# Attention and a gated MLP on one core: q without zero padding, w_in converted in halves throughout, and two slices of w_in loaded through ScalarE's DMA queue

## The chip, the cores and the metric

One core of a Trainium2 chip runs the whole program in one launch. The metric is device microseconds of an execution; the median of three executions stands for the kernel. Engines are called as in the profile: PE (TensorE), PEld (its weight loads), DVE (VectorE), ACT (ScalarE), POOL (GpSimd) and SP (SyncE, which here only issues DMAs).

## The reference

q, k and v are 4 batches x 12 heads x 448 positions x 64. The attention is causal; its output, as 1792 tokens x 768, goes through a gated MLP with w_in (768 x 2048) and w_out (2048 x 768). Both weights arrive as 64-bit floats, q, k and v as 32-bit ones; the output is float32.

```python
scores = scale * np.matmul(q, k.transpose(0, 1, 3, 2))
scores = np.where(mask, -1000000000.0, scores)
attn = np.exp(scores - np.max(scores, axis=-1, keepdims=True))
attn = attn / (np.sum(attn, axis=-1, keepdims=True) + 1e-09)
x = concat_heads(np.matmul(attn, v))
h = x @ w_in
g = h * (1.0 / (1.0 + np.exp(-1.702 * h)))
out = g @ w_out
```

## The kernel before

**Work.** Each batch's 448 positions are cut into blocks of 256 and 192 (eight blocks in all), each block into chunks of 64 positions. A *unit* is a block and a pair of heads: six units to a block. For each unit, scores of each chunk go to PSUM on TensorE (`scores_of`, L1071), DVE adds the mask and takes the row's minimum of the negated scores (L1112), ACT takes the exponential (L1126), the weights are scaled by the reciprocal of their sum, turned, and multiplied with v (L1268) into xT. Then comes the MLP of that block: `h_slice` (L412 with ps_h) over eight slices of w_in of 256 columns, the gate on ACT and DVE, and `out_tile` (L1405) with w_out. MLP products take each operand as a high and a low half-precision part, so w_in and w_out are converted and split on the chip.

**The first batch in float32.** For batch 0 the six units of both blocks work in float32 (`f32`, L853). `q_unit32` (L917) and `k_unit32` (L900) load two heads as 128 (or 96) rows, TensorE turns them into ps_o (`turn`, L885, matmuls at L893), and a copy by ACT or DVE (`scaled`, L472 or L474) brings them to SBUF. In kT the two heads lie in the upper and lower 64 partitions, copied at once. In qT each head has its own 64 columns of a 128-wide group, and the other head's half of these partitions is zero: four memsets (L934) write the zeros once, and each unit needs two copies of 64 partitions. The scores of a chunk are then a product over all 128 partitions, issued by `halves` (L408 to L412) as two matmuls of 64 stationary columns each, the zeros removing the other head. A run of two chunks shares a PSUM bank if it has at most 512 columns; the first block of a batch has two such groups for a unit, the second three (320, 384 and 448 columns).

**w_in.** `w_in_slice` (L632) loads a slice of 64-bit words in two DMAs of 768 KB on SP's queue (L648), into one of two raw buffers in wob (slices s and s + 2 share one). `to_f32` (L551) turns it into float32 with four operations: a scaling on ACT (L472), two 16-bit operations on DVE (L574, which may run on ACT as L566, and L588), and one on DVE (L599) that reads the raw words for the last time. The first three slices (`early=3`) do this in two halves, each after its own DMA; the others in one piece after both. Then follow the products of a slice with itself on TensorE, a maximum, a scale, and the split into two parts (L472 or L474, and L477).

**Order.** Every instruction is added to `Ops` with a price, its engine or engines of choice, and a priority. `Ops.order` searches 600 times, starting from a seed, for the order in each engine's queue with the least planned time (`forward`, `backward` and `late`), with prices such as `LOAD` for the issue of a DMA on SP, and the program is then emitted in that order. All loads go through SP's one queue, in the planned order. `warm` (L529) makes ACT load its table at the start.

The planner's price for the float32 scores, which the change leaves, is

```python
add({"PE": (4 * o / 2.4 + 6 * len(run)) / 1e3}, scores32, [qt_key] + kt_keys, bank(sb), prio)
```

with o the columns of the group, in nanoseconds for both halves together.

Of the kernel before, what the change touches and what calls it, by code (L numbers as in the profile page):

```python
# [11 lines left out]
F32 = mybir.dt.float32  # L12
# [36 lines left out]
    va=2,  # L49
    ub=(0.0, 60.0, 122.92, 9.75),  # L50
    wi2=2.63,
    early=3,
)

SEED = 2


class Ops:
# [5 lines left out]

    ENGINES = ("SP", "PE", "ACT", "DVE", "POOL")
    HOP = 0.14
    SECOND = 1e5
    LOAD = 0.68  # L70
    DMA_START, DMA_END, DMA_DEPTH = 1.23, 1.6, 8
    ROWS = 0.195

# [50 lines left out]
    def late(self, result, rnd):  # L124
        free = dict.fromkeys(self.ENGINES, 0.0)
        end = [0.0] * len(self.ops)
        bus, flying, clock = 0.0, [], Clock()
        for i, e in result:
            costs, _, deps, _, dma = self.ops[i]
            start = max([free[e]] + [end[d] + self.HOP for d in deps])  # L130
            if e == "SP":
                start = max([start] + flying[-self.DMA_DEPTH :][: len(flying) // self.DMA_DEPTH][:1])
                free[e] = start + costs[e]
                bus = max(bus, start + self.DMA_START) + dma
                end[i] = bus + self.DMA_END + 0.8 * rnd.random()
                flying.append(end[i])
                continue
            if e == "PE":
                end[i] = clock.after(start, costs[e])
            else:  # L140
                end[i] = start + costs[e] * (1 + 0.03 * rnd.random()) + (0.15 * rnd.random() if e == "POOL" else 0.0)
            free[e] = end[i]
        return max(free.values())

    def backward(self, found, spread, rnd):
        _, result, fin = found
        n = len(self.ops)
        on = dict(result)
        key = [-fin[i] - (rnd.gauss(0.0, spread) if spread else 0.0) for i in range(n)]
        wait, left = [0] * n, [0.0] * n  # L150
        for o in self.ops:
            for d in o[2]:
                wait[d] += 1
        ready = {e: [] for e in self.ENGINES}
        free = dict.fromkeys(self.ENGINES, 0.0)
        coming = [(0.0, i) for i in range(n) if not wait[i]]
        heapify(coming)
        at, now, done = [0.0] * n, 0.0, 0
        while done < n:
            while coming and coming[0][0] <= now + 1e-9:  # L160
                _, i = heappop(coming)
                heappush(ready[on[i]], (key[i], i))
            moved = False
            for e in self.ENGINES:
                if free[e] > now + 1e-9 or not ready[e]:
                    continue
                _, i = heappop(ready[e])
                costs, _, deps, _, dma = self.ops[i]
                left[i] = free[e] = now + costs[e]
                if e == "SP":  # L170
                    free[e] = now + max(costs[e], dma)
                    left[i] = now + self.DMA_START + dma + self.DMA_END + 0.3
                moved = True
                done += 1
                for d in deps:
                    at[d] = max(at[d], left[i] + self.HOP)
                    wait[d] -= 1
                    if not wait[d]:
                        heappush(coming, (at[d], d))
            if not moved:  # L180
                times = [free[e] for e in self.ENGINES if free[e] > now + 1e-9 and ready[e]]
                if coming:
                    times.append(coming[0][0])
                now = max(min(times), now)
        end = max(left)
        return [end - x for x in left]

    def forward(self, prios):
# [8 lines left out]
        coming = [(0.0, i) for i in range(n) if not wait[i]]  # L197
        taken = [None] * n
        free = dict.fromkeys(self.ENGINES + ("BULK",), 0.0)
        bus = 0.0  # L200
        clock = Clock()
        flying = []
        at = [0.0] * n
# [2 lines left out]
        while len(result) < n:  # L206
# [8 lines left out]
            for e in ("BULK",) + self.ENGINES:  # L215
# [11 lines left out]
                free[e] = end = now + costs[e]  # L227
                if e == "PE":
                    free[e] = end = clock.after(now, costs[e])
                if e == "SP":  # L230
                    go = max([now] + flying[-self.DMA_DEPTH :][: len(flying) // self.DMA_DEPTH][:1])
                    free[e] = go + costs[e]
                    bus = max(bus, go + self.DMA_START) + dma
                    end = bus + self.DMA_END
                    flying.append(end)
                    free["BULK"] = max(free["SP"], bus - TUNE["slack"])
# [76 lines left out]
def kernel(  # L313
# [76 lines left out]
    def col(tag, n=2, w=1):  # L390
        if tag not in col_at:
            col_at[tag] = (col_used[0], Ring(n))
            col_used[0] += n * w
            assert col_used[0] <= 175
        o, ring = col_at[tag]
        i = ring.next()
        return cols[:, o + i * w : o + (i + 1) * w], ("col", tag, i)
# [133 lines left out]
        nc.scalar.activation(out=cols[:, 175:], in_=cols[:, 175:], func=AF.Exp)  # L531

    add(dve(1), lambda e: nc.vector.memset(cols[:, 175:], 0.0), [], ["warm"], -2e6)
    add({"ACT": 1.5}, warm, [], ["warm"], -2e6)

    def zero_v(prio):
        add(
# [94 lines left out]
    def w_in_slice(s, prio):  # L632
# [11 lines left out]
        src = w_in32[:, 2 * s * WS : 2 * (s + 1) * WS].rearrange("(k p) f -> p k f", p=P)  # L644
        for h in range(2):
            add(
                {"SP": Ops.LOAD},
                lambda e, h=h: nc.sync.dma_start(  # L648
                    out=raw.bitcast(I32).rearrange("p (k w) -> p k w", k=NU)[:, 3 * h : 3 * h + 3],
                    in_=src[:, 3 * h : 3 * h + 3],  # L650
                ),
# [203 lines left out]

    ident = cp.tile([P, P], F32, name="ident")
    ident_keys = ["ident"]
    stale = [True] * 2
    ps_t_r = Ring(2)

    def identity(e):
# [55 lines left out]
    def q_unit32(n, u, prio):  # L917
# [6 lines left out]
        load_heads(f, q[b, 2 * u : 2 * u + 2, 64 * c0 : 64 * c1], r, [[x] for x in keys], prio, 0.062 * ni)  # L924
        got, got_key = turn(f, r, keys, prio)
        t = qT_r.next()
        qt = qT[t].rearrange("p c w -> p (c w)").bitcast(F32).rearrange("p (c j w) -> p c j w", j=2, w=64)
        key = ("qT", t)
        if stale[t]:
            stale[t] = False  # L930
            for j in range(2):
                add(
                    {"POOL": 0.4},
                    lambda e, j=j: nc.gpsimd.memset(qt[64 * j : 64 * j + 64, :, 1 - j], 0.0), [], [key], prio - 1,  # L934
                )
        for j in range(2):
            add(
                {**act(64 * ni, psum=True, rate=1.0), **dve(64 * ni)},
                lambda e, j=j: scaled(
                    e,  # L940
                    qt[64 * j : 64 * j + 64, :ni, j].rearrange("p c (x t) -> p c x t", t=2),
                    got[64 * j : 64 * j + 64].rearrange("p (c x) t -> p c x t", c=ni),
                    1.0,
                ),
                [got_key], [key], prio,
            )
        return qt[:, :ni], key, -QK_SCALE, None

    def k_pair(b, u, prio):

# [101 lines left out]
    def q_unit(n, u, prio):  # L1052
# [4 lines left out]
        if u % 2 == 0:  # L1057
            q_pair(n, u, prio)
        t, m = qT_r.next(), u % 2
        stale[t] = True  # L1060
        add(
            Ops.turned(2 * ni),
            lambda e: nc.sync.dma_start_transpose(out=qT[t][:, : 2 * ni], in_=q16[:, m * 256 * ni : (m + 1) * 256 * ni]),
# [7 lines left out]
    def scores_of(n, u, run, qt, qt_key, prio):  # L1071
# [8 lines left out]

        def scores32(e):
            for i, ps in zip(run, places):
                halves(ps, qt[:, i - c0].rearrange("p j w -> p (j w)"), kt[:, : 64 * (i + 1)], True, True)

        def scores(e):
            for i, ps in zip(run, places):
# [410 lines left out]
    moe(NB - 1)  # L1497

    with tc.manual_schedule():
        for i, e in ops.order():  # L1500
            ops.ops[i][1](e)


# [30 lines left out]
```

## Time and profile before

| | |
|---|---|
| three executions | 603.63, 605.53, 605.74 us (median 605.53) |
| the profiled execution | 605.29 us, its span 603.5 us |
| busy share of the span | PE 95%, PEld 83%, DVE 69%, ACT 58%, POOL 10% |
| granted TensorE clock, mean | 0.994 |
| DMA | 79.90 MB, mean 132 GB/s |

The times are of executions without and with a profile; the span runs from the first to the last instruction. A matmul's end is modelled, so that a busy PE may still have gaps inside; idle time of PE is real. The DMA share of a stretch is the mean over 16 DMA engines and can come out a little above 1. In the rows below, "idle" with an arrow names what ended the wait.

### The profile page before, as it was taken

What the parts mean: (1) busy time and instruction counts of PE and PEld (TensorE: products, weight loads), DVE (VectorE), ACT (ScalarE), POOL (GpSimd) and SP (SyncE); (2) the same over time, 40 slices, a digit from 0 to 9 for tenths busy, and PEclk for the clock granted to TensorE, in tenths of its full rate; (3) what the DMA queues carried; (4) which work ended last, traced back from release to release, by engine and by line L of the source; (5) the groups of instructions that cost most, each with busy time, mean ns of one, the idle gap of its engine ahead of it and who ended that gap; (6) DMA issues with size and microseconds to landing.
All of it is one profiled execution on the core that took longest, in us unless ns stands there. A gap on an engine that the chain in (4) does not pass through costs nothing.

```text
span 603.5 us, 22259 instructions
## 1 busy us (share of the span) xinstructions
PE 575.1 (95%) x9526; PEld 501.7 (83%) x9526; DVE 416.6 (69%) x1164; ACT 351.6 (58%) x835; POOL 59.2 (10%) x162
## 2 busy tenths in 40 slices
PE   3876999999999999999999999999999999999997
PEld 2555867886699799977888899998999999889986
DVE  2999999999996889977489887978777122203100
ACT  4888899887866767754676465666355122203110
POOL 3000000012120121212111210211100000000000
PEclk9989899999999999999999999999999999999999
DMA  8998478554498987899997899575835400000000
GB/s 270 277 288 281 128 251 302 173 127 110 86 177 156 142 163 112 167 176 153 156 158 115 155 161 174 105 128 120 130 59 68 94 2 15 1 28 3 28 28 27
DMA packets 201604, 79.90 MB, mean 132 GB/s; under 512 B 182304, under 2 KB 191264, under 8 KB 201504
## 3 DMA queue, kind: packets, MB, share of 16 engines
q1 hardware_dynamic: 201504, 78.47, 61.5%
q8 instruction: 74, 1.21, 0.9%
q14 instruction: 26, 0.21, 0.1%
HBM read 41.68 MB, written 5.51 MB: 78 GB/s over the span
## 4 chain that ended last, share of the span: by engine, by line
PE 68%; DVE 4%; ACT 2%; DMA 1%; issue 1%; SPq 0%; DVEq 0%; ACTq 0%
PE ps_o L1405 33%; PE ps_h L412 26%; PE ps_s L1089 4%; PE ps_v L1268 4%; DVE z L1112 1%; DMA vraw<-in_v_dram 1%; ACT p L472 1%; PE ps_s L412 1%; DVE p L477 1%; PE ps_h L883 1%; DVE ps_h L1367 0%; ACT waste L462 0%; DMA kf<-in_k_dram 0%; DVE q L477 0%; DVE gT L477 0%
## 5 line engine op out<-in xcount | busy, mean ns | idle before, releaser
L412 PE MATMUL ps_h<-xT,wib 128*64 128x256 f16 (+1 forms) x4608 | 244.4, 260 | 0.1
L1405 PE MATMUL ps_o<-wob,gT 128*64 128x384 f16 x2688 | 239.8, 326 | 0.8 <-DVE wob L477 0.6
L412 PEld LDWEIGHTS <-wib 128*64 128x64 f16 x4608 | 226.3, 110 | 7.9 <-issue 2.1
L1405 PEld LDWEIGHTS <-gT 128*64 128x64 f16 x2688 | 171.8, 110 | 38.3 <-issue 3.2
L1126 ACT ACTIVATE z<-z,cols 128x320 f32<-128x320 f32 (+6 forms) x168 | 84.1, 501 | 51.6 <-DVE cols L1112 49.1
L1367 DVE SCALAR_TENSOR_TENSOR ps_h<-t,ps_h 128x512 f32<-128x512 f32 (+1 forms) x64 | 40.1, 626 | 82.4 <-ACT t L1362 82.0
L1362 ACT ACTIVATE t<-ps_h,cols 128x512 f32<-128x512 f32 (+1 forms) x64 | 40.3, 629 | 72.1 <-PE ps_h L412 68.0
L1112 DVE CUSTOM_DVE_ANT_0 z<-ps_s,mask,cols 128x128 f32<-128x128 f32 (+6 forms) x126 | 57.2, 479 | 18.0 <-PE ps_s L1089 17.4
L477 DVE SCALAR_TENSOR_TENSOR p<-z,cols,p 128x128 f16<-128x128 f32 (+3 forms) x126 | 63.2, 528 | 1.5 <-ACT p L472 0.8
L477 DVE SCALAR_TENSOR_TENSOR gT<-ps_h,gT 128x512 f16<-128x512 f32 (+1 forms) x64 | 39.7, 620 | 13.5 <-ACT gT L472 13.1
L1268 PE MATMUL ps_v<-PT,v 128*64 128x192 f16 (+7 forms) x792 | 44.7, 257 | 0.5 <-DVE cols L453 0.4
L1089 PE MATMUL ps_s<-kT,qT 128*64 128x64 f16 (+4 forms) x504 | 41.5, 273 | 1.2 <-DVE cols L1112 0.9
L472 ACT ACTIVATE p<-z,cols 128x384 f16<-128x384 f32 (+3 forms) x66 | 34.0, 533 | 13.3 <-DVE cols L1235 9.7
L472 ACT ACTIVATE gT<-ps_h 128x512 f16<-128x512 f32 (+1 forms) x53 | 28.9, 545 | 20.4 <-DVE ps_h L1367 20.3
L472 ACT ACTIVATE ob<-ps_o,cols 128x384 f32<-128x384 f32 x24 | 13.8, 577 | 45.0 <-PE ps_o L1405 44.6
L1126 ACT ACTIVATION_READ_ACCUMULATOR z<-z,cols 128x1 f32 x168 | 31.6, 188 | 0.0
L412 PE MATMUL ps_s<-kT,qT 128*64 128x320 f32 (+6 forms) x168 | 25.0, 409 | 5.6 <-DVE cols L1112 5.6
L1268 PEld LDWEIGHTS <-v 128*64 128x64 f16 x648 | 29.2, 110 | 1.0
L1089 PEld LDWEIGHTS <-qT 128*64 128x64 f16 x504 | 24.7, 110 | 4.3 <-issue 1.3
L1047 POOL TENSOR_SCALAR q<-q 128x512 f16<-128x512 f16 (+1 forms) x32 | 21.9, 686 | 50.8 <-ACT q L472 26.6
L474 DVE TENSOR_SCALAR p<-z,cols 128x256 f16<-128x256 f32 (+3 forms) x60 | 24.6, 422 | 1.3
L472 ACT ACTIVATE wob<-wob 128x768 f32<-128x768 f32 (+1 forms) x20 | 21.8, 1091 | 5.5 <-DMA wob<-in_moe_w_in_dram 5.0
(98 smaller groups left out, 564.9 us busy)
## 6 DMA issues: line engine op xcount, KB each, us to landing
wob<-in_moe_w_in_dram SPq DMA_DIRECT2D x16, 768.0 KB, 6.5
wob<-in_moe_w_out_dram SPq DMA_DIRECT2D x9, 768.0 KB, 6.2
vraw<-in_moe_w_out_dram SPq DMA_DIRECT2D x7, 768.0 KB, 6.7
out_dram<-ob SPq DMA_DIRECT2D x28, 192.0 KB, 2.2
kf<-in_k_dram SPq DMA_DIRECT2D x36, 112.0 KB, 3.3
vraw<-in_v_dram SPq DMA_DIRECT2D x9, 384.0 KB, 5.0
qf<-in_q_dram SPq DMA_DIRECT2D x48, 64.0 KB, 3.1
qf<-in_q_dram SPq DMA_DIRECT2D x48, 48.0 KB, 3.2
```

The source lines that it names most:

```text
L412: nc.tensor.matmul(out[o : o + 64], lhsT[:, o : o + 64], rhs, start=start, stop=stop)
L472: nc.scalar.activation(out=dst, in_=src, func=AF.Copy, scale=sc)
L474: nc.vector.tensor_scalar(out=dst, in0=src, scalar1=sc, scalar2=None, op0=ALU.mult)
L477: nc.vector.scalar_tensor_tensor(out=dst, in0=src, scalar=sc, in1=hi, op0=ALU.mult, op1=ALU.subtract)
L1047: nc.gpsimd.tensor_scalar(out=dst, in0=src, scalar1=1.0, scalar2=1.0, op0=ALU.mult, op1=ALU.mult)
L1089: nc.tensor.matmul(ps[64 * j : 64 * j + 64], qt[:, g, i - c0, 64 * j : 64 * j + 64], kt[:, : i + 1, 64 * j : 64 * j + 64], start=(g == 0), ...
L1112: lambda e: nc.vector.tensor_tensor_reduce(out=z[:, :w], in0=ps, in1=mask[:, S - w :], scale=c, scalar=3.0e38, op0=ALU.add, op1=ALU.min, a ...
L1126: lambda e: nc.scalar.activation(out=z[:, :w], in_=z[:, :w], func=AF.Exp, bias=m, scale=-1.0, accum_out=l),
L1268: nc.tensor.matmul(ps[64 * j : 64 * j + 64, 64 * (first - c0) : w], vt[:, J, j] if f32(b, u) else vt[:, gv, J, j, :], (p_f32(pi)[:, at] if ...
L1362: lambda e: nc.scalar.activation(out=th, in_=ph, func=AF.Tanh, scale=ts[:, sl : sl + 1]),
L1367: lambda e: nc.vector.scalar_tensor_tensor(out=ph, in0=th, scalar=1.0, in1=ph, op0=ALU.add, op1=ALU.mult),
L1405: nc.tensor.matmul(po[64 * j : 64 * j + 64, :OH], gT[:, f, gg, 64 * r : 64 * r + 64], wo_pair(f, gw, nh), start=(f == 0 and gg + gw == 0), ...
```

## The change

- The q of the float32 units loses its zeros: qT holds the two heads in the upper and the lower 64 partitions, as kT does, copied at once for all 128 partitions. The memsets and the `stale` flags go. The scores of a chunk are two matmuls over 64 partitions each, one for a head: partitions 0 to 63 to the PSUM partitions 0 to 63, and 64 to 127 to 64 to 127.
- `early` goes from 3 to 8: all slices of w_in are converted in halves.
- The loads of the first two slices of w_in (`beside=2`, four DMAs) are issued by ACT on its own DMA queue, ahead of everything else. The planner gets this queue as an engine AQ, with `BESIDE` as the factor on transfers while both queues are at work. The price of `warm` grows by the four issues.
- `LOAD` goes from 0.68 to 0.5 and the seed from 2 to 3; the order is searched anew.

```diff
-    early=3,
+    early=8,
+    beside=2,
...
-SEED = 2
+SEED = 3
...
-    LOAD = 0.68
+    LOAD = 0.5
+    BESIDE = 1.4
...
+            if e == "AQ":
+                free[e] = start + costs[e]
+                side = max(side, start + self.DMA_START) + self.BESIDE * dma
+                end[i] = side + self.DMA_END + 0.8 * rnd.random()
+                continue
...
-                bus = max(bus, start + self.DMA_START) + dma
+                bus = max(bus, start + self.DMA_START)
+                bus += dma * (self.BESIDE if bus < side else 1.0)
...
-    add({"ACT": 1.5}, warm, [], ["warm"], -2e6)
+    add({"ACT": 1.5 + 2 * Ops.LOAD * TUNE["beside"]}, warm, [], ["warm"], -2e6)
...
-                {"SP": Ops.LOAD},
-                lambda e, h=h: nc.sync.dma_start(
+                {"AQ" if s < TUNE["beside"] else "SP": Ops.LOAD},
+                lambda e, h=h: (nc.scalar if e == "AQ" else nc.sync).dma_start(
...
-        qt = qT[t].rearrange("p c w -> p (c w)").bitcast(F32).rearrange("p (c j w) -> p c j w", j=2, w=64)
+        qt = qT[t].rearrange("p c w -> p (c w)").bitcast(F32)[:, : 64 * ni]
         key = ("qT", t)
-        if stale[t]:
-            stale[t] = False
-            for j in range(2):
-                add(
-                    {"POOL": 0.4},
-                    lambda e, j=j: nc.gpsimd.memset(qt[64 * j : 64 * j + 64, :, 1 - j], 0.0), [], [key], prio - 1,
-                )
-        for j in range(2):
-            add(
-                {**act(64 * ni, psum=True, rate=1.0), **dve(64 * ni)},
-                lambda e, j=j: scaled(
-                    e,
-                    qt[64 * j : 64 * j + 64, :ni, j].rearrange("p c (x t) -> p c x t", t=2),
-                    got[64 * j : 64 * j + 64].rearrange("p (c x) t -> p c x t", c=ni),
-                    1.0,
-                ),
-                [got_key], [key], prio,
-            )
-        return qt[:, :ni], key, -QK_SCALE, None
+        add(
+            {**act(64 * ni, psum=True, rate=1.2), **dve(64 * ni, rate=1.2)},
+            lambda e: scaled(e, qt.rearrange("p (x t) -> p x t", t=2), got, 1.0),
+            [got_key], [key], prio,
+        )
+        return qt, key, -QK_SCALE, None
...
-                halves(ps, qt[:, i - c0].rearrange("p j w -> p (j w)"), kt[:, : 64 * (i + 1)], True, True)
+                for j in range(2):
+                    x = slice(64 * j, 64 * j + 64)
+                    nc.tensor.matmul(
+                        ps[x], qt[x, 64 * (i - c0) : 64 * (i - c0) + 64], kt[x, : 64 * (i + 1)], start=True, stop=True
+                    )
...
-        for i, e in ops.order():
+        for i, e in sorted(ops.order(), key=lambda x: x[1] != "AQ"):
```

## Rows read from the trace of the kernel before

**Rows 1.** Busy us of each engine by stretch: (x instructions), TensorE clock, DMA share, GB/s

```profile
0.00:5.00 5.00, 0.00 (x0) 0.00 (x0) 0.06 (x1) 1.49 (x2) 3.84 (x20) 1.00 0.45 128
5.00:10.00 5.00, 1.80 (x10) 1.04 (x10) 1.47 (x3) 2.50 (x4) 0.71 (x4) 1.00 1.07 333
10.00:15.00 5.00, 3.49 (x28) 2.92 (x30) 2.45 (x8) 3.19 (x6) 0.00 (x0) 1.00 1.05 349
15.00:64.50 49.50, 38.09 (x520) 27.33 (x518) 47.21 (x146) 40.33 (x103) 0.00 (x0) 0.94 0.96 288
64.50:200.00 135.50, 132.88 (x2186) 108.77 (x2184) 125.15 (x333) 115.59 (x249) 13.57 (x31) 1.00 0.68 162
200.00:590.00 390.00, 388.74 (x6674) 353.32 (x6670) 240.25 (x677) 187.34 (x472) 41.07 (x109) 1.00 0.57 100
590.00:603.50 13.50, 10.04 (x124) 8.34 (x120) 0.00 (x0) 1.16 (x2) 0.00 (x0) 1.00 0.09 30
```

**Rows 2.** The timeline of the first 15 us: start, us, engine, line, operation

```profile
0.80 0.87 SPq L875 DMA_DIRECT2D q<-in_k_dram  x2
...
1.72 0.43 SPq L648 DMA_DIRECT2D wob<-in_moe_w_in_dram  x1
...
2.19 0.96 SPq L875 DMA_DIRECT2D qf<-in_q_dram  x2
...
6.76 0.89 ACT L472 ACTIVATE wob<-wob 128x768 f32<-128x768 f32 x1 [4.47 <-DMA wob<-in_moe_w_in_dram]
...
7.26 1.12 PE L893 MATMUL ps_o<-ident,qf 128*64 128x128 f32 x8 [7.26 <-DMA qf<-in_q_dram]
...
8.42 0.42 DVE L474 TENSOR_SCALAR qT<-ps_o 64x256 f32<-64x256 f32 x1 [7.49 <-PE ps_o L893]
...
11.04 1.11 PE L893 MATMUL ps_o<-ident,q 128*64 128x128 f32 x6 [1.05 <-DMA q<-in_k_dram]
...
14.55 0.23 DVE L1112 CUSTOM_DVE_ANT_0 z<-ps_s,mask 128x64 f32<-128x64 f32 x1 [1.96 <-PE ps_s L412]
```

**Rows 3.** Instructions on the tile qT: duration min/median/max in ns

```profile
L472 ACT ACTIVATE qT<-ps_o x17: 303/327/380, 8.9 to 112.2; 64x192 f32<-64x192 f32 x9, 64x256 f32<-64x256 f32 x8
L474 DVE TENSOR_SCALAR qT<-ps_o x7: 350/399/428, 8.4 to 54.6; 64x256 f32<-64x256 f32 x4, 64x192 f32<-64x192 f32 x3
```

**Rows 4.** Groups by shape, 0 to 62 us: copies of kT (busy us, mean ns)

```profile
L472 ACT ACTIVATE kT<-ps_o 128x256 f32<-128x256 f32 x6 | 2.3, 377 | 1.8 <-PE ps_o L893 1.8
...
L472 ACT ACTIVATE kT<-ps_o 128x192 f32<-128x192 f32 x4 | 1.3, 322 | 0.9 <-PE ps_o L893 0.9
```

**Rows 5.** Groups by shape, 0 to 62 us: conversion of w_in

```profile
L472 ACT ACTIVATE wob<-wob 128x1536 f32<-128x1536 f32 x4 | 6.5, 1621 | 0.0
...
L599 DVE SCALAR_TENSOR_TENSOR wob<-wob 128x768 int32<-128x768 int32 x6 | 5.7, 947 | 0.4 <-ACT wob L566 0.3
...
L472 ACT ACTIVATE wob<-wob 128x768 f32<-128x768 f32 x6 | 5.4, 907 | 5.0 <-DMA wob<-in_moe_w_in_dram 5.0
...
L599 DVE SCALAR_TENSOR_TENSOR wob<-wob 128x1536 int32<-128x1536 int32 x3 | 5.3, 1753 | 0.0
...
L574 DVE TENSOR_SCALAR wob<-wob 128x1536 uint16<-128x1536 uint16 x4 | 4.2, 1050 | 0.0
...
L574 DVE TENSOR_SCALAR wob<-wob 128x768 uint16<-128x768 uint16 x4 | 2.4, 598 | 0.0
```

**Rows 6.** TensorE's timeline around two groups of matmuls, between 100 and 130 us

```profile
103.76 0.52 PE L412 MATMUL ps_o<-wob 128*64 128x128 bf16 x12
104.11 0.93 PE L412 MATMUL ps_s<-kT,qT 128*64 128x448 f32 x4
104.86 0.52 PE L412 MATMUL ps_o<-wob 128*64 128x128 bf16 x12
...
127.22 0.55 PE L412 MATMUL ps_o<-wob 128*64 128x128 bf16 x12
127.70 0.66 PE L883 MATMUL ps_h<-ident,z 128*128 128x128 f32 x4
```

More of the change, by code (lines that the diff above doesn't have):

```diff
@@ L51 @@
     wi2=2.63,
-    early=3,
+    early=8,
+    beside=2,
 )
-SEED = 2
+SEED = 3
 class Ops:
-    ENGINES = ("SP", "PE", "ACT", "DVE", "POOL")
+    ENGINES = ("SP", "AQ", "PE", "ACT", "DVE", "POOL")
     HOP = 0.14
     SECOND = 1e5
-    LOAD = 0.68
+    LOAD = 0.5
+    BESIDE = 1.4
     DMA_START, DMA_END, DMA_DEPTH = 1.23, 1.6, 8
@@ L126, in late @@
         end = [0.0] * len(self.ops)
-        bus, flying, clock = 0.0, [], Clock()
+        bus, side, flying, clock = 0.0, 0.0, [], Clock()
         for i, e in result:
@@ L169, in backward @@
                 left[i] = free[e] = now + costs[e]
-                if e == "SP":
+                if e in ("SP", "AQ"):
                     free[e] = now + max(costs[e], dma)
@@ L199, in forward @@
         free = dict.fromkeys(self.ENGINES + ("BULK",), 0.0)
-        bus = 0.0
+        bus = side = 0.0
         clock = Clock()
@@ L229, in forward @@
                     free[e] = end = clock.after(now, costs[e])
+                if e == "AQ":
+                    side = max(side, now + self.DMA_START) + self.BESIDE * dma
+                    end = side + self.DMA_END
                 if e == "SP":
@@ L232, in forward @@
                     free[e] = go + costs[e]
-                    bus = max(bus, go + self.DMA_START) + dma
+                    bus = max(bus, go + self.DMA_START)
+                    bus += dma * (self.BESIDE if bus < side else 1.0)
                     end = bus + self.DMA_END
@@ L393, in col @@
             col_used[0] += n * w
-            assert col_used[0] <= 175
+            assert col_used[0] <= 174
         o, ring = col_at[tag]
@@ L857 @@
     ident_keys = ["ident"]
-    stale = [True] * 2
     ps_t_r = Ring(2)
@@ L1059, in q_unit @@
         t, m = qT_r.next(), u % 2
-        stale[t] = True
         add(
```

## The prediction

> **What bounds the kernel now.** I read the busy times by stretch first [rows 1]. From 64.5 to 590 us TensorE leaves 2.62 + 1.26 = 3.9 us idle out of 525.5; the last 13.5 us hold another 3.5. Before 64.5 us it is idle for 5 + 3.2 + 1.5 + 11.4 = 21.1 us. So the end is set by the moment from which TensorE always has work, and what can be won lies almost all in the first 64.5 us. In that stretch the second column to see is DVE: from 15 to 64.5 us it is busy 47.21 of 49.5 us (95%), ACT 40.33 (81%), and from 64.5 to 200 us still 125.15 of 135.5 (92%) and 115.59 (85%). It is DVE, with ACT close behind, that hands TensorE its operands. Before 15 us DVE is busy only 0.06 + 1.47 + 2.45 = 4.0 us: 11 us are lost there. The DMA engines, at a share of 0.45 in the first 5 us, are full from 5 to 15 us (1.07 and 1.05) and nearly so after (0.96).
>
> The timeline of the first 15 us, read next, says what DVE waits for [rows 2]. SP issues two loads of k at 0.80, half a slice of w_in (768 KB) at 1.72, and q only behind it at 2.19; TensorE turns q at 7.26, DVE copies it at 8.42. The second k comes behind a further half slice, TensorE turns it at 11.04, and the first softmax chunk starts on DVE at 14.55. ACT meanwhile starts on w_in at 6.76. Small loads that attention needs at once stand behind large ones in one queue.
>
> **The change, term by term.** The sum is made against the profiled execution: span 603.5 us, time 605.3 us, 0.2 below the median of 605.5.
>
> *Four w_in loads on ACT's queue.* They are issued ahead of everything on ACT: 4 x 0.43 us, the price of such an issue on SP [rows 2], = 1.7 us, before an engine that is busy 1.49 us in the first 5 us and then waits until 6.76; that wait hides them, and without it they would cost 1.7 us of ACT. SP's own issues behind them move up by as much. What is gained: 786 KB at the 333 to 349 GB/s of 5 to 15 us [rows 1] are 2.3 us. One half slice no longer stands before the first q, one more not before the second k. So DVE's first copy could come 2.3 us earlier (6.1) and its first chunk 4.6 us earlier (9.9). Bounds: 4.6 us, both delays in full; and nothing, because the engines are full from 5 us on and the w_in halves, now sharing them, come later by what q and k gain. Attention's work then fills DVE's gaps while w_in is on its way: 10 to 15 us has 2.55 us of DVE idle, 5 to 10 us some 0.5 us that 2.3 us earlier would reach. I take -3.0 us, nearer to the favourable end because those idle rows hold it. The slices from the third on stay in SP's queue and wait, as now, for a raw buffer.
>
> That the two queues are one resource behind the issue is also a rule: the Trainium skill ("DMA: Bandwidth & Descriptors", Issuing engines are not separate DMA queues) says that loads issued from several engines run on the same 16 DMA engines, and that only issue time is saved. By it this term would be the 1.7 us of issues, and the sum 1.3 us higher.
>
> *q in one copy.* 17 copies on ACT and 7 on DVE go [rows 3]: 17 x 0.327 + 7 x 0.399 = 8.4 us (medians). Twelve copies of 128 partitions take their place. The copies of kT have that shape: 6 x 0.377 + 6 x 0.322 = 4.2 us [rows 4]. 4.2 us of two nearly full engines are saved; bounds 0 (all of it on an idle moment of ACT) and -4.2. As the planner may give a copy to either, half of it counts: -2.1. The four POOL memsets, on an engine that is idle from 10 us on [rows 1], cost nothing: the first copy waits for TensorE [rows 2], not for them, and if it comes at 6.1 us their absence keeps it free.
>
> *w_in converted in halves.* For five more slices ACT's 1.62 us becomes 2 x 0.907, and on DVE 1.75 becomes 2 x 0.947 and 1.05 becomes 2 x 0.598, twice (L588 does the same amount as L574) [rows 5]. That is +0.19 us of ACT and 0.14 + 2 x 0.15 = +0.44 us of DVE for a slice, 3.2 us for five. A half frees its buffer earlier, but the loads are ahead of the conversions there, so I give nothing for it. Bounds 0 (the first half runs while the second lands) and +3.2; half, as above: +1.6.
>
> *The 64-row quadrants on TensorE.* The number of matmuls, columns and weight loads is the same, two matmuls for a chunk. The present pair runs side by side: a chunk of 448 columns takes 104.86 - 104.11 = 0.75 us [rows 6], which at 2.4 GHz is 4 cycles a column for both halves, just what the planner's price counts for one. No row shows a 64-row tile. Bounds: 0, if the quadrants run side by side as the two halves do; at the other end, one after the other, they double their time, 1152/448 x 0.75 = 1.93 us for the three long chunks of a unit, 11.6 us for the six units (the four short chunks lie mostly before 64.5 us, where TensorE has slack). I take 0: the two tiles share neither rows nor columns, even less than the two halves do.
>
> *Prices, seed.* LOAD, BESIDE and the seed only give another order. It cannot win more than the 3.9 us idle after 64.5 us, and I give it as much to lose; taken: 0.
>
> **Sum:** -3.0 - 2.1 + 1.6 = -3.5: 605.3 - 3.5 = 601.8, and 602.0 against the median. I predict 602.0. About 0.5% (3 us, so 602.5 to 608.5 is "the same") is what a measurement of this kernel can tell from no change.
>
> **Rivals.**
>
> 1. *A switch of tile form eats it.* When TensorE goes from 128*64 tiles to 128*128 ones, a visible gap appears: twelve matmuls of ps_o last 104.11 - 103.76 = 0.35 us before another 128*64 group but 127.70 - 127.22 = 0.48 before the transposes [rows 6]: 0.13 us. If a 64-row tile is such another form, each group of scores pays twice, 0.26 us. Six units have three groups each in the second block, 18 x 0.26 = 4.7 us in the stretch in which TensorE has no slack. 601.8 + 4.7 = 606.5, the same. For it: the gap is there. Against: those transposes change the number of columns, the quadrants only that of rows. Chance 0.22. The Trainium skill ("TensorEngine Tiling (Array Packing)", Key Properties) states it in general: changing the tiling mode drains TensorE.
>
> 2. *The DMA engines are the limit.* Shares of 1.07 and 1.05 from 5 to 15 us leave nothing to win; w_in comes later by what q and k gain, DVE is as late as now. Only the other terms stay: 605.3 - 2.1 + 1.6 = 604.8, the same. Against: it is not bytes that DVE lacks before 15 us but the right ones. Chance 0.17.
>
> 3. *Slower: the quadrants serialize.* Both write one PSUM bank. If the second waits for the first, the 11.6 us above fall on a TensorE that leaves only 2.6 us idle from 64.5 to 200 us: 601.8 + 11.6 = 613.4. It turns slower from about 7 us on, that is, if over 60% of the overlap is lost. Against: the two halves write one bank now, on the same two sets of partitions, and overlap. Chance 0.10. The Trainium skill (same page, Gotcha 1: PSUM Pressure) says that different row tiles cannot access one bank at the same time.
>
> 4. *Slower: a worse order.* The new order leaves the 3.9 us in place and adds as much again, at a start that is not better: 605.3 + 3.9 = 609.2. Nothing in the rows speaks for it. Chance 0.08.
>
> **Chances and range.** The forecast (faster by over 0.5%) 0.43; within 0.5%: 0.22 + 0.17 = 0.39; slower by over 0.5%: 0.10 + 0.08 = 0.18. All terms at their good ends give 605.3 - 4.6 - 4.2 = 596.5; start and copies at nothing with conversions in full 608.5. Not all ends are met together: 597 to 609 holds the forecast and the first two rivals, nearly touches the fourth and leaves out the third and the tails. The forecast's own range is 597 to 602.5.
>
> **What would show it.** Right: q is turned near 5 us instead of 7.26; the first chunk on DVE starts near 10 instead of 14.55, with DVE busy over 5 us before 15; TensorE has full work from about 61 instead of 64.5 us; twelve copies of q with 128 partitions; 0.75 us from a chunk of 448 columns to the next group. Rival 1: that step is 0.9 to 1.0 us, and TensorE's weight loads show gaps around the scores. Rival 2: ACT's first conversion moves from 6.76 to 9 us or later, and DVE's idle time before 15 us stays near 11 us. Rival 3: 1.5 us for that chunk. I am wrong if the first 64.5 us shorten and the time does not: then a stage after 64.5 us got longer, through TensorE's gaps or the order.

## The result: 0.6% slower

Ten executions of the changed kernel took 604.69 to 610.22 us, median 608.6, beside ten of the kernel before with a median of 604.76: ratio 1.0060, 95% interval 1.0043 to 1.0076, some 3.6 us. Twelve more executions later gave 607.75 beside 604.84 (1.0044, 1.0025 to 1.0064). The forecast was 602.0 us with a range to 609: the time lies inside, the sign is wrong.

One caution for reading the profile: the profiled execution is the fastest of the ten, 604.69 us with a span of 602.6. Its rows say what each step became; the difference between medians is taken from the runs. The profile of the repetition (606.07 us) has the same features.

The busy times by stretch, profile of the changed kernel, columns as in [rows 1]:

```profile
0.00:5.00 5.00, 0.00 (x0) 0.00 (x0) 0.06 (x1) 0.00 (x0) 3.43 (x18) 1.00 0.52 172
5.00:10.00 5.00, 1.98 (x16) 1.60 (x16) 0.00 (x0) 1.21 (x1) 0.00 (x0) 1.00 1.03 305
10.00:15.00 5.00, 3.77 (x28) 2.44 (x30) 2.99 (x10) 2.96 (x10) 0.00 (x0) 1.00 1.06 348
15.00:64.50 49.50, 37.56 (x512) 24.20 (x510) 47.83 (x162) 46.22 (x113) 0.00 (x0) 0.95 0.98 288
64.50:200.00 135.50, 135.00 (x2184) 107.55 (x2180) 120.34 (x316) 112.57 (x246) 16.53 (x32) 0.99 0.68 160
200.00:590.00 390.00, 389.83 (x6694) 351.88 (x6690) 243.01 (x685) 188.03 (x468) 39.74 (x109) 1.00 0.58 101
590.00:603.50 13.50, 9.09 (x112) 7.58 (x108) 0.00 (x0) 1.16 (x2) 0.00 (x0) 0.97 0.08 29
```

TensorE's idle time from 64.5 to 590 us fell from 3.9 to 0.5 + 0.2 = 0.7 us, yet TensorE is no further: from 64.5 to 200 us about as much work (2184 matmul records, 2186 before) fills 135.00 busy us instead of 132.88. A part of that is TensorE's clock, of which 1.00 stands for 2.4 GHz and 0.50 for 1.2. Before, then changed:

```profile
64.50:70.00 5.50, 5.50 (x98) 4.70 (x96) 5.50 (x20) 5.25 (x8) 0.00 (x0) 0.95 0.52 79
...
64.50:70.00 5.50, 5.50 (x57) 2.98 (x52) 4.58 (x13) 4.42 (x8) 0.00 (x0) 0.80 0.30 69
```

TensorE is busy throughout in both, so 5.5 x (0.95 - 0.80) = 0.8 us of its full speed are lost there, by estimate. More goes to the 64-row scores (below). Before 64.5 us TensorE wins nothing: 21.2 us idle against 21.1, and DVE is busy 3.05 us in the first 15 us, less than the 3.98 before. ACT works only 4.2 us of the first 15 (7.2 before) and makes up for it after: 46.2 us from 15 to 64.5, instead of 40.3.

The timeline of the start (as [rows 2]; ACTq is ACT's issuing of loads):

```profile
0.79 7.97 ACTq L660 DMA_DIRECT2D wob<-in_moe_w_in_dram  x4
...
1.25 0.89 SPq L886 DMA_DIRECT2D qf<-in_q_dram  x2
...
7.96 1.12 PE L904 MATMUL ps_o<-ident,qf 128*64 128x128 f32 x8 [7.96 <-DMA qf<-in_q_dram]
...
8.79 1.28 ACT L543 ACT_TABLE_LOAD   x1 [8.79 <-DMA wob<-in_moe_w_in_dram]
...
10.19 0.37 ACT L484 ACTIVATE qT<-ps_o 128x256 f32<-128x256 f32 x1
10.46 0.89 ACT L484 ACTIVATE wob<-wob 128x768 f32<-128x768 f32 x1
...
13.42 0.29 DVE L1113 CUSTOM_DVE_ANT_0 z<-ps_s,mask 128x128 f32<-128x128 f32 x1
```

ACT's four issues last from 0.79 to 8.76 us, not 1.7 us. The table load follows at 8.79, the first copy at 10.19, the first conversion of w_in at 10.46 instead of 6.76. q is turned at 7.96 instead of 7.26, although it was issued earlier. The first softmax chunk starts on DVE at 13.42 instead of 14.55, 1.1 us earlier where I took up to 4.6.

TensorE's timeline around two score groups:

```profile
94.41 1.17 PE L424 MATMUL ps_h<-xT,wib 128*64 128x256 f16 x18
95.51 0.97 PE L1082 MATMUL ps_s<-kT,qT 64*64 64x448 f32 x4
96.41 1.17 PE L424 MATMUL ps_h<-xT,wib 128*64 128x256 f16 x18
97.42 0.51 PE L424 MATMUL ps_o<-wob 128*64 128x128 bf16 x12
```

and TensorE's weight loads in the same stretch:

```profile
95.51 0.19 PEld L1082 LDWEIGHTS ps_s<-kT,qT 64*64 64x64 f32 x4 [0.20 <-issue]
96.41 0.91 PEld L424 LDWEIGHTS <-wib 128*64 128x64 f16 x18 [0.70 <-issue]
```

The chunk of 448 columns takes 96.41 - 95.51 = 0.90 us to the next group, 0.75 before [rows 6], and the 18 matmuls ahead of it 95.51 - 94.41 = 1.10 us; ahead of another 128*64 group such 18 take 97.42 - 96.41 = 1.01. The weight loads stand still for 0.20 us ahead of the scores; the 0.70 us behind them is mostly the scores' own time. So the quadrants do run side by side (one after the other would take 1.5 us), and a visit between groups of 128*64 tiles costs a switch in and a switch out, about 0.1 us and 0.15 us.

### The profile page after: what moved, and what is told of

The parts are those of the page before. It is cut to its first block, busy times and chain, and to the rows that moved or that the text cites. A ratio compares the mean times of both kernels' runs of the same rounds, so it can differ in the third digit from the quotient of the medians.

```text
span 602.6 us, 22274 instructions
## 1 busy us (share of the span) xinstructions
PE 577.2 (96%) x9526; PEld 495.2 (82%) x9526; DVE 414.2 (69%) x1171; ACT 352.1 (58%) x836; POOL 59.7 (10%) x158
## 4 chain that ended last, share of the span: by engine, by line
PE 90%; DVE 4%; ACT 2%; DMA 2%; issue 1%; ACTq 0%; DVEq 0%
PE ps_h L424 37%; PE ps_o L1406 36%; PE ps_v L1269 5%; PE ps_s L1090 5%; PE ps_s L1082 3%; PE ps_h L894 2%; PE ps_o L424 2%; DMA wob<-in_moe_w_in_dram 1%; DMA PT<-p 1%; PE ps_o L904 1%; DVE wib L489 1%; DVE wob L611 1%; ACT z L1127 1%; DVE wob L600 1%; DVE z L1113 1%
## 5 line engine op out<-in xcount | busy, mean ns | idle before, releaser
L1406 PEld LDWEIGHTS <-gT 128*64 128x64 f16 x2688 | 169.1, 110 | 38.3 <-issue 2.1
L1127 ACT ACTIVATE z<-z,cols 128x320 f32<-128x320 f32 (+5 forms) x168 | 84.1, 502 | 47.0 <-DVE cols L1113 44.4
L1113 DVE CUSTOM_DVE_ANT_0 z<-ps_s,mask,cols 128x64 f32<-128x64 f32 (+6 forms) x126 | 57.0, 479 | 13.2 <-PE ps_s L1090 12.6
L1269 PE MATMUL ps_v<-PT,v 128*64 128x192 f16 (+7 forms) x792 | 43.1, 251 | 0.2 <-DMA PT<-p 0.2
L484 ACT ACTIVATE p<-z,cols 128x512 f16<-128x512 f32 (+3 forms) x65 | 34.0, 537 | 13.2 <-DVE cols L1236 8.6
L1082 PE MATMUL ps_s<-kT,qT 64*64 64x320 f32 (+6 forms) x168 | 26.9, 428 | 2.9 <-ACT kT L484 1.4
L1230 POOL TENSOR_SCALAR cols<-cols 128x2 f32<-128x2 f32 (+1 forms) x49 | 14.0, 285 | 132.2 <-ACT z L1127 131.7
L1045 POOL TENSOR_SCALAR q<-q 128x384 f16<-128x384 f16 (+1 forms) x31 | 20.6, 665 | 60.0 <-ACT q L484 40.9
```

The costliest lines, as they stand in the source:

```text
L484: nc.scalar.activation(out=dst, in_=src, func=AF.Copy, scale=sc)
L1082: nc.tensor.matmul(ps[x], qt[x, 64 * (i - c0) : 64 * (i - c0) + 64], kt[x, : 64 * (i + 1)], start=True, stop=True)
L1113: lambda e: nc.vector.tensor_tensor_reduce(out=z[:, :w], in0=ps, in1=mask[:, S - w :], scale=c, scalar=3.0e38, op0=ALU.add, op1=ALU.min, a ...
L1127: lambda e: nc.scalar.activation(out=z[:, :w], in_=z[:, :w], func=AF.Exp, bias=m, scale=-1.0, accum_out=l),
L1269: nc.tensor.matmul(ps[64 * j : 64 * j + 64, 64 * (first - c0) : w], vt[:, J, j] if f32(b, u) else vt[:, gv, J, j, :], (p_f32(pi)[:, at] if ...
L1406: nc.tensor.matmul(po[64 * j : 64 * j + 64, :OH], gT[:, f, gg, 64 * r : 64 * r + 64], wo_pair(f, gw, nh), start=(f == 0 and gg + gw == 0), ...
```

## The experiments

Ratios are to the kernel before on the same chip, with 95% intervals; 0.1% is 0.6 us. *In the order of* a kernel means that this kernel's planned order is used and only what an instruction does, or the place of a few loads, is replaced, so that no newly searched order mixes in.

**The 64-row scores, alone and undone.** First in the order of before, q still padded and copied twice:

```diff
-  halves(ps, qt[:, i - c0].rearrange("p j w -> p (j w)"), kt[:, : 64 * (i + 1)], True, True)
+  for j in range(2):
+      x = slice(64 * j, 64 * j + 64)
+      nc.tensor.matmul(ps[x], qt[x, i - c0, j], kt[x, : 64 * (i + 1)], start=True, stop=True)
```

> The kernel before in its own order, with the scores as two matmuls over 64 rows and nothing else changed. Switch theory: 3.5 to 4.7 us slower than before, a step of 0.90 us from a 448-column chunk to the next group and 0.11 to 0.13 us more before it. Rival that the quadrants cost nothing: no difference.

Measured 1.0046 (1.0028 to 1.0064), 2.8 us slower, less than the 3.5 to 4.7 expected. Its timeline of TensorE shows the two gaps in a stretch that [rows 6] show without:

```profile
105.08 0.51 PE L412 MATMUL ps_o<-wob 128*64 128x128 bf16 x12
105.52 0.97 PE L1085 MATMUL ps_s<-kT,qT 64*64 64x448 f32 x4
106.42 0.54 PE L412 MATMUL ps_o<-wob 128*64 128x128 bf16 x12
```

Twelve matmuls of ps_o take 105.52 - 105.08 = 0.44 us before the scores instead of 0.35, the 448-column chunk 0.90 instead of 0.75: 0.24 us for this visit. Not every visit costs as much. The last score group stands between transposes of 128*128 tiles, where the tile form changes in any case. Before, then with 64 rows:

```profile
153.01 0.97 PE L412 MATMUL ps_s<-kT,qT 128*64 128x448 f32 x4
153.92 0.66 PE L883 MATMUL ps_h<-ident,z 128*128 128x128 f32 x4
...
155.49 0.97 PE L1085 MATMUL ps_s<-kT,qT 64*64 64x448 f32 x4
156.39 0.66 PE L883 MATMUL ps_h<-ident,z 128*128 128x128 f32 x4
```

Here the step is 0.91 and 0.90 us: nothing is added. For all sixteen groups past 61 us I added up two steps: from the start of the last matmul ahead of a group to its first, and from there to the next matmul behind it. With 64 rows they are 3.05 us longer in the sum than before, which agrees with the 2.8 us measured.

Then the reverse, in the order of the changed kernel: zeros in q (written by POOL at the start), two copies at the place of the one (not shown here), `halves` again.

```diff
+  nc.gpsimd.memset(z[64 * j : 64 * j + 64, :, 1 - j], 0.0)
...
-  nc.tensor.matmul(
-      ps[x], qt[x, 64 * (i - c0) : 64 * (i - c0) + 64], kt[x, : 64 * (i + 1)], start=True, stop=True
-  )
+  halves(ps, qt[:, i - c0].rearrange("p j w -> p (j w)"), kt[:, : 64 * (i + 1)], True, True)
```

> The changed kernel in its own order, with q zero padded again and scores over 128 rows (two copies in the place of one). Theory that the 64-row tiles cost a switch each way: 3.5 to 4.7 us faster than the changed kernel, less up to 1 us for the twelve extra copies. Rival, that the new order or the start is what costs: within 1 us of the changed kernel or slower.

Measured 1.0031 (1.0016 to 1.0046). Against the changed kernel (1.0044 and 1.0060) that looks 0.8 to 1.7 us faster, less than expected, and the intervals overlap. The traces show two opposite parts. The same sixteen groups past 61 us take 2.9 us less with zeros (the same two steps, added up). But the kernel with zeros, which carries twelve copies more, comes to them later: the instruction that DVE starts at 61.3 us in the changed kernel it starts 3.0 us later. The third kernel was to price these copies: compact q and 64-row scores as changed, but copied in two instructions of 64 partitions.

```diff
-  lambda e: scaled(e, qt.rearrange("p (x t) -> p x t", t=2), got, 1.0),
+  lambda e: [
+      scaled(
+          e,
+          qt[64 * j : 64 * j + 64].rearrange("p (x t) -> p x t", t=2),
+          got[64 * j : 64 * j + 64],
+          1.0,
+      )
+      for j in range(2)
+  ],
```

> The changed kernel in its own order and with its 64-row scores, but q copied twice, 64 partitions each time. Theory that the joint copy is worth its engine time: 12 more copies of 0.33 to 0.38 us, ACT 4 to 5 us busier in the first 110 us, 1 to 2 us slower than the changed kernel. Rival that the copies were hidden: no difference.

Measured 1.0112 (1.0087 to 1.0137): 4.9 us slower than the version with zeros, which has the same order and as many copies, and 3.1 to 4.1 us slower than the changed kernel, where 1 to 2 were expected. Neither number is a price, for TensorE's speed differs at the start. With zeros, then with two copies:

```profile
19.31 0.66 PE L908 MATMUL ps_o<-ident,q 128*64 128x128 f32 x8 [0.59 <-ACT qT L484]
21.46 0.29 DVE L640 TENSOR_REDUCE cols<-ps_o 128x1 f32<-128x128 f32 x1 [1.26 <-PE ps_o L424]
...
19.60 1.12 PE L904 MATMUL ps_o<-ident,q 128*64 128x128 f32 x8 [0.35 <-ACT qT L484]
23.88 0.29 DVE L640 TENSOR_REDUCE cols<-ps_o 128x1 f32<-128x128 f32 x1 [3.25 <-PE ps_o L424]
...
35.76 1.12 PE L904 MATMUL ps_o<-ident,q 128*64 128x128 f32 x8
```

Eight matmuls of a turn take 0.66 us in the one and 1.12 in the other, which comes to 0.71 only at 25.65 us. They take 1.12 us again at 35.76, where the granted clock is 0.55 (35 to 40 us); before 25 us the clock column reads 1.00 all the same. At the same instructions of DVE the kernel with two copies is level with the one with zeros at 17.7 us, 3.4 us behind it at 27.6 and 4.1 us at 68.3. So most of the 4.9 us is lost ahead of the groups on a full TensorE. Why TensorE stayed slow so long in this run is not shown, and it prices neither the 64-row scores nor the joint copy. The sums over sixteen groups do price the scores, at some 3 us in either order, and in the order of the changed kernel the two halves of the q part nearly cancel.

The q part alone (one copy, no memsets, 64-row scores) in the order of before:

```diff
-  lambda e, j=j: scaled(
-      e,
-      qt[64 * j : 64 * j + 64, :ni, j].rearrange("p c (x t) -> p c x t", t=2),
-      got[64 * j : 64 * j + 64].rearrange("p (c x) t -> p c x t", c=ni),
-      1.0,
-  ),
+  lambda e, j=j: None if j else scaled(e, qt.rearrange("p (x t) -> p x t", t=2), got, 1.0),
```

> The kernel before in its own order with the q part of the change alone: one copy of 128 partitions at the place of the first of the two, no memsets, scores over 64 rows. From the two runs that took the part apart in the changed kernel's order (scores over 64 rows +4.6 us, one copy for two -3.6 us): 0 to 2 us slower than before, faster than the 607.7 us of the 64-row scores with two copies. Rival that the q part is a gain in this order: 1 us or more faster than before.

Measured 1.0029 (1.0018 to 1.0039), 1.8 us slower. With two copies it was 2.8: there the joint copy looks worth about 1 us (these two intervals overlap). The q part is a loss.

**The second queue.** Four loads on ACT's queue ahead of everything, in the order of before (`first` holds their places):

```diff
-  lambda e, h=h: nc.sync.dma_start(
+  lambda e, h=h: (nc.scalar if s < 2 else nc.sync).dma_start(
...
-  for i, e in ops.order():
+  for i, e in sorted(ops.order(), key=lambda x: x[0] not in first):
```

> The kernel before in its own order, the first four loads of w_in on ACT's queue ahead of everything. Theory that ACT stands still until the third load is taken: ACT's table load near 8.8 us instead of 0.8, its first conversion near 10 instead of 6.8, no gain, 0 to 1.5 us slower. Rival that the earlier q and k win: 1.5 to 3 us faster.

Measured 1.0053 (1.0038 to 1.0067), 3.2 us slower, more than the theory's 1.5. With one slice, `s < 1`, that is two loads:

> The kernel before in its own order, only the first slice of w_in (two loads) on ACT's queue ahead of everything. Theory that ACT's standstill is the loss: ACT's table load starts near 1.8 us, its first conversion before 8 us, and of the 3.1 us that four loads cost at most 1 us is left. Rival that sharing the DMA engines is the loss: ACT is free early and the time is still 2 to 3 us over before.

Measured 1.0013 (0.9996 to 1.0030), 0.8 us, within the theory. The starts of both, four loads first:

```profile
0.79 8.62 ACTq L650 DMA_DIRECT2D wob<-in_moe_w_in_dram  x4
...
8.82 1.12 PE L897 MATMUL ps_o<-ident,qf 128*64 128x128 f32 x8 [8.82 <-DMA qf<-in_q_dram]
9.44 1.28 ACT L531 ACT_TABLE_LOAD   x1 [9.44 <-DMA v<-in_v_dram]
...
10.84 0.86 ACT L472 ACTIVATE wob<-wob 128x768 f32<-128x768 f32 x1
```

and with two:

```profile
0.79 1.01 ACTq L650 DMA_DIRECT2D wob<-in_moe_w_in_dram  x2
...
1.83 1.28 ACT L531 ACT_TABLE_LOAD   x1 [1.83 <-issue]
...
5.86 0.88 ACT L472 ACTIVATE wob<-wob 128x768 f32<-128x768 f32 x1 [2.53 <-DMA wob<-in_moe_w_in_dram]
...
8.94 1.12 PE L897 MATMUL ps_o<-ident,qf 128*64 128x128 f32 x8 [8.94 <-DMA qf<-in_q_dram]
```

With two loads ACT goes on at 1.83 us and converts from 5.86; with four it stands until 9.44. One and the same instruction of DVE, before, with four and with two loads:

```profile
18.53 0.28 DVE L628 TENSOR_REDUCE cols<-ps_o 128x1 f32<-128x128 f32 x1
...
21.03 0.28 DVE L628 TENSOR_REDUCE cols<-ps_o 128x1 f32<-128x128 f32 x1
...
19.47 0.28 DVE L628 TENSOR_REDUCE cols<-ps_o 128x1 f32<-128x128 f32 x1
```

With four loads it starts 2.5 us later than before, with two 0.9, not far from what the whole runs lose (3.2 and 0.8). So the standstill looks like the larger part; the two runs differ in the bytes on the second queue as well, and the two causes cannot be told apart here. And q is turned at 8.94 and 8.82 us in the two, later than the 7.26 of before, although it is issued at 1.72 instead of 2.19: the DMA engines, with the w_in loads of the other queue, move 176 and 168 GB/s in the first 5 us (128 before) and are full from 5 to 10 (a share of 1.12 in both, 1.07 before). The Trainium skill ("DMA: Bandwidth & Descriptors", Issuing engines are not separate DMA queues), which lets a second issuing engine save issue time only, agrees with these rows; the standstill took even the issue time back.

Two milder versions, in the order of the changed kernel. The third and fourth issue behind ACT's table load and first copy (`beside` holds the four loads, `rest_of` all else, `second` the place of that copy):

```diff
-  for i, e in sorted(ops.order(), key=lambda x: x[1] != "AQ"):
...
+  for i, e in beside[:2] + rest_of[: second + 1] + beside[2:] + rest_of[second + 1 :]:
```

> The changed kernel in its own order, ACT's third and fourth load issued behind its table load and its first copy, so that these don't wait for the queue. Theory that the blocked ACT delays the start: ACT's first copy at 9.1 instead of 10.2 us, TensorE's full work 1 us earlier and the time 0.5 to 1 us less. Rival, that the start is set by the DMA engines: no difference.

Measured 1.0034 (1.0017 to 1.0051). The table load moves to 1.83 us, but the first copy only to 9.96, not 9.1: it waits for TensorE's turn, which waits for q, still at 7.95. The two late issues then hold ACT for 1.99 us from 9.97. And all four loads on SP, ahead of its second, fifth, ninth and twelfth own load:

```diff
-  lambda e, h=h: (nc.scalar if e == "AQ" else nc.sync).dma_start(
+  lambda e, h=h: nc.sync.dma_start(
...
+  if e == "SP" and n < 12:
+      if n in (1, 4, 8, 11):
+          j, f = beside.pop(0)
+          ops.ops[j][1](f)
+      n += 1
```

> The changed kernel in its own order, the four loads of the first two slices of w_in on SP's queue among its first twelve loads. Theory that ACT's queue wins nothing, since the DMA engines are full and ACT stands still until the third load is taken: 0 to 1.5 us faster than the changed kernel. Rival that the second queue brings the start forward: 1.5 to 3 us slower.

Measured 1.0037 (1.0022 to 1.0051). Both point the way expected and neither is clear of the changed kernel's own intervals.

**The halves.** Slices 3 to 7 converted whole, at the place of the second half, in the order of the changed kernel (a load that would overwrite the raw half too early is held until then; `fns` holds the operations on a whole slice, a and b are the places of the halves):

```diff
+  ops.ops[a] = (ops.ops[a][0], lambda e: None) + ops.ops[a][2:]
+  ops.ops[b] = (ops.ops[b][0], fns[x]) + ops.ops[b][2:]
```

> The changed kernel in its own order, slices 3 to 7 of w_in converted in one piece at the place of the second half. Theory that the halves cost 3.2 us of DVE and ACT of which half counts: 1 to 1.6 us faster than the changed kernel. Rival that they overlap with loads and win: 0.5 to 2 us slower.

Measured 1.0121 (1.0097 to 1.0144): 3.7 to 4.7 us slower than the changed kernel, the contrary of what I expected. That order was made for halves, and TensorE's clock was lower too (0.88 from 15 to 64.5 us, 0.95 in the changed kernel), so it does not show what halves win over an order made for whole slices. Their price alone, in the order of before, two halves right behind each other (`fns` holds the four operations for the first half and for the second):

```diff
+  for x in range(4):
+      o = ops.ops[base + x]
+      ops.ops[base + x] = (o[0], lambda e, x=x: [fns[x](e), fns[4 + x](e)]) + o[2:]
```

> The kernel before in its own order, each conversion operation of slices 3 to 7 issued as two halves, one right behind the other, both still after both loads. It holds the price of the halves (+0.19 us of ACT and +0.44 us of DVE a slice, 3.2 us for five) without what an earlier start can win. Theory that this time counts by half or more: 1.6 to 3.2 us slower than before. Rival that the price is hidden: within 0.8 us.

Measured 1.0028 (1.0007 to 1.0048), 1.7 us with 0.4 to 2.9 open. And the halves alone with a new order, `early=8` in the kernel before, with three seeds:

> The kernel before with all slices of w_in converted in halves, the order searched anew with its own seed. Theory that the halves win: 1 to 3 us faster than the mean of the three orders of the kernel before (604.4, 606.9, 607.6: 606.3), that is 603.3 to 605.3. Rival that they cost 1.6 us: near 608.

> The same with seed 3, beside the kernel before with seed 3 (606.9). Theory that the halves win: 603.5 to 605.5. Rival that they cost 1.6 us: 608.5.

> The kernel before with all slices in halves and seed 4, beside the kernel before with seed 4 (607.6). If the halves themselves win 1 to 3 us: 604.5 to 606.5. If only the order of the own seed was lucky: 607 to 610, and the mean of three orders with halves no lower than that of three orders without (606.3).

Measured 0.9970 (0.9954 to 0.9987), 1.0099 (1.0082 to 1.0116) and 1.0014 (0.9997 to 1.0030). The first, median 601.82 us, beats both kernels and what was expected of it. The second, 610.56, missed its expectation by 5 us. The third, 605.82, came where a gain by the halves was to put it.

**The order.** Other seeds for the kernel before (`SEED = 2` made 3 and 4) and the changed one (`SEED = 3` made 2 and 4), nothing else changed:

> The kernel before with the seed of the changed one: how far apart two orders of one program lie. Theory: within 1.5 us of the kernel before. Rival that the order is what counts: 2.5 us or more slower, as much as the whole change.

> The kernel before with a third seed. Theory that the seed of before is a good draw and others lie 1 to 3 us above: 606 to 608 us. Rival that seed 3 was a bad draw: within 1 us of the kernel before.

> The changed kernel with the seed of before, hence another order of the same instructions. Theory that order is worth little against the tile switches: within 1.5 us of the changed kernel, still over the kernel before. Rival that the order found is what costs: 2.5 us or more away from the changed kernel.

> The changed kernel in a third order. Theory that the orders of one program spread by 2 to 3 us: 605.5 to 609.5, and the mean of three orders of the changed kernel within 1.5 us of the mean of three orders of the kernel before (606.3). Rival that the change itself costs 3 to 4 us in any order: 609 to 611.

| seed | before | changed | before with halves |
|---|---|---|---|
| 2 | 1 | 1.0046 | 0.9970 |
| 3 | 1.0041 | 1.0060 and 1.0044 | 1.0099 |
| 4 | 1.0035 | 1.0030 | 1.0014 |
| mean | 1.0025 | 1.0043 | 1.0028 |

Before with seeds 3 and 4 has intervals of 1.0028 to 1.0053 and 1.0018 to 1.0052; the changed kernel with seeds 2 and 4 of 1.0027 to 1.0065 and 1.0014 to 1.0047. Before with seed 3 was expected within 1.5 us of before and came out 2.5 us slower; the other three lie where they were expected. So the order of before was the best of its three by 2.1 to 2.5 us, and over three orders each the programs differ by 0.2%, less than their orders do. Among orders with halves the spread is 1.3%, 7.8 us. The changed kernel itself, once more:

> The changed kernel once more, for a second trace. Theory (tile switches cost 4.7 us on TensorE, the early start is not won): again 3.5 to 4.5 us over the kernel before. If the first profile's 604.7 us is the truth and the others are chance: no difference.

It gave 1.0044, 2.7 us, a little under what was expected.

Where the good order with halves has its gain can be read at its start:

```profile
0.80 0.87 SPq L875 DMA_DIRECT2D qf<-in_q_dram  x2
...
1.72 0.42 SPq L875 DMA_DIRECT2D q<-in_k_dram  x1
...
2.19 0.91 SPq L875 DMA_DIRECT2D qf<-in_q_dram  x2
...
2.75 1.51 PE L893 MATMUL ps_o<-ident,qf 128*64 128x128 f32 x8 [2.75 <-POOL one L508]
...
3.13 0.43 SPq L875 DMA_DIRECT2D q<-in_k_dram  x1
...
3.61 0.43 SPq L648 DMA_DIRECT2D wob<-in_moe_w_in_dram  x1
...
12.39 0.29 DVE L1112 CUSTOM_DVE_ANT_0 z<-ps_s,mask 128x128 f32<-128x128 f32 x1 [0.40 <-PE ps_s L412]
```

In this order SP issues six loads of q and k ahead of anything large, two of q first, and half a slice of w_in only as the seventh load, at 3.61. TensorE turns q at 2.75, and the first chunk is on DVE at 12.39. That is the early start I had credited to the second queue, got in one queue by order. From 10 to 15 us DVE is busy 4.49 us (2.45 before), but hardly ahead of that: over the first 15 us it is 4.56 against 3.98.

```profile
10.00:15.00 5.00, 4.53 (x40) 3.94 (x42) 4.49 (x13) 2.44 (x8) 0.00 (x0) 1.00 1.10 343
```

Up to 64.5 us TensorE has 594 matmul records, against 554 before. That the start is the reason for its 1.8 us was not tried by itself, and a rival is open: the good order has a granted clock of 1.00 from 60 to 65 us, where the kernel before has 0.67: up to 5 x 0.33 = 1.6 us of TensorE's full speed, by estimate.

## Why the prediction was wrong, point by point

- **The quadrants, taken at 0: the step that failed first.** I argued that tiles without common rows or columns disturb each other even less, and took the end of the range that says so. They do run side by side, so rival 3 is out (0.90 us, not 1.5). But a 64-row tile is another tile form, as rival 1 said, and a score group among 128*64 tiles pays a switch in and out, 0.24 us. Measured: 2.8 us in the order of before. Rival 1's 4.7 us is too much, since it charged 0.26 us to all 18 groups of the second block; past 61 us there are sixteen, those beside transposes pay less, and the sum is 3.05 us, or 2.9 in the order of the changed kernel. The trace agrees with the Trainium skill ("TensorEngine Tiling (Array Packing)", Key Properties) that a change of the tiling mode drains TensorE: 0.24 us a visit among 128*64 tiles. The Trainium skill's sentence on one PSUM bank for two row tiles (same page, Gotcha 1: PSUM Pressure) does not show here as lost time.
- **The start, taken at -3.0: wrong, and for a reason not on my list.** I priced four issues on ACT at SP's 0.43 us each and called them hidden. SP's row for a first load said nothing of a third one in the same queue, which is taken only at 7.84 us. ACT, which unlike SP has work of its own, stood still for 8 us. The signs of rival 2 came true: ACT's first conversion moved to 10.46 us, DVE was idle for 12 of the first 15, and q came later, not earlier. But the rival blamed the DMA engines alone, and ACT's standstill had a part. In the order of before four such loads cost 3.2 us; in the order of the changed kernel, taking them off ACT wins 0.4 to 1.4 us, which is not clear of nothing.
- **One copy for two, taken at -2.1: right in sign, its size open.** About 1 us in one order, with overlapping intervals. In the other, where the planner had put all twelve on ACT, the kernel with zeros and two copies is 3.0 us later at 61 us; the copies are not the only difference there (its clock is 0.83 from 25 to 30 us). The memsets' price of nothing rested on a POOL that is idle from 10 us on; [rows 1] show that up to 64.5 us only, which is enough for it.
- **The halves, taken at +1.6: the price fits**, 1.7 us in place, with 0.4 to 2.9 open, so that it fits partly by luck. Whether their earlier start wins more than that stays open: one order says yes, the mean of three (1.0028 against 1.0025) says neither.
- **Prices and seed, taken at 0 with 3.9 us either way: mis-sized.** The order of before was a good draw, 2.1 to 2.5 us under two others, and a change that makes the planner search anew gives such a draw up. For the changed kernel's 3.6 us this alone would be more than half. That is rival 4, held at 0.08, at a smaller size. One order with halves lies 6.0 us above before, with the price of the halves in it.
- **TensorE's clock, in no term and no rival.** It takes some 0.8 us from 64.5 to 70 us in the changed kernel's profile, and a longer slow start decides the run with two copies. What of the differences between orders is clock was not tried.
- **Added up:** in the order of before the q part (+1.8) and the queue (+3.2), each measured alone, lose 5.0 us; against three orders of before, three orders of the changed kernel are 1.1 us slower on the mean, which three draws each cannot tell from nothing. How the 3.6 us divide between parts and order in the very order that was run stays open, and so does what the slower of its executions lose beyond the profiled one: its span, 602.6 us, is shorter than the 603.5 of before.

## What to carry to other kernels

A matmul in another tile form is not free because its columns are: look for the gap beside the nearest change of form in the trace, and multiply it by the visits on a full TensorE whose neighbours have another form. A load issued by a compute engine can stop that engine until the queue takes it, as the third of four did here, so look in the trace at how many go out at once; small urgent loads come early by standing first in one queue. Where a planner draws the order anew, compare several draws of both programs, or keep the order, before a part of a change is given credit. And where two runs differ, look first at how long the same matmuls take at the start of both: a slower TensorE can look like a price.

## What the runs showed of the hardware that was not expected

ACT's queue took two loads of 768 KB at once (0.79 and 1.3 us) and the third only at 7.84, with the engine's own instructions waiting behind it; with two loads on it, the engine went on at 1.83. With large loads on a second queue the small ones came later: q, issued at 1.25 us with four large loads beside it, was turned at 7.96, and issued at 0.80, first in one queue, at 2.75. And two half-height tiles on the diagonal of the array, writing different partitions of one PSUM bank, work at the same time (0.90 us for 448 columns, 0.75 for two 128*64 tiles). TensorE's first matmuls were slow, where the clock column reads 1.00: eight of a turn took 1.03 us at 14.68 and 0.66 at 16.68 in the changed kernel, and still 1.12 at 19.60 with two copies.
